# RWKV attention feeding two mixtures of experts, on one core: the attention's small products regrouped by the part of the matmul array they use, and a new hand-written order of the steps

## Chip, core and metric

One NeuronCore of one Trainium2 chip runs the whole program in one launch. The metric is the device time in microseconds (us). Before the change the median of three runs is 1038.5 us.

## What is computed

```python
for t in range(S):                                   # attention, S = 768, 2 batches, 8 heads of 48
    cur = einsum('bhd,bhe->bhde', u[None] * kt, vt)
    y[:, :, t] = einsum('bhd,bhde->bhe', rt, state + cur)
    state = wt[..., None] * state + einsum('bhd,bhe->bhde', kt, vt)
...
P = exp(x @ w_gate - max)                            # first mixture: 8 rounds of row and column
for _ in range(8):                                   # normalisation, then all 8 experts on all rows
    P /= P.sum(1, keepdims=True) + 1e-09; P /= P.sum(0, keepdims=True) + 1e-09; P *= N / E
for e in range(E):
    out += P[:, e:e+1] * (maximum(x @ w1[e], 0) @ w2[e])
...
expert_idx = argmax(xn @ en.T / tau)                 # second mixture: the best expert alone
```

There are 1536 rows of 384 numbers; an expert's two weight matrices are 384 x 1024 and 1024 x 384.

## The kernel before

The attention works in 12 chunks of 128 time steps, six to a batch (`CPB` is 6, so chunks 0 and 6 begin with an empty state). Within a chunk the recurrence is turned into matrix products. Two heads share the 128 partitions: one has partitions 0 to 47, the other 64 to 111, and four such pairs lie side by side.

Each chunk c passes through steps, named in a list by a letter and the chunk's number. `b`, `a` and `c` are DVE work alone (decays by two scans, and the scaled keys `Kt`, queries `Rh` and the product `rp`). The others issue TensorE products:

- `C` (att1d): the bonus term, 16 products with 32 columns of weights each (L639).
- `d` (att2): the scores, 8 products of 48 rows with 128 columns of weights (L654), then 4 transposes of `Kt` (L657); DVE masks the scores into `AT`, ScalarE copies the transposes to `KtT`, GpSimd scales the state `St` to `Tt` (L667).
- `f` (att3): the state's share of the output, 16 products of 48 rows with 64 columns of weights (L679; not in chunks 0 and 6), then the scores' share, 32 products with 32 columns of weights (L686); DVE adds up `x` (L693).
- `z` (att3z): the state's update, 8 products with 48 columns of weights (L718); DVE adds `Tt` and writes `St` (L723).
- `g` (att4): 3 transposes of `x` (L730) and their copies; `h` (att5): the gate's logits, 12 products with 32 columns of weights (L771).

A product of plain float32 operands shows as two rows of weight load and two of matmul in the trace, so `f` issues 64 matmuls from 32 products. The weights of a product are its second operand in the names (`ps<-Rh,Kt`: the weights are `Kt`).

Between these steps stand pieces of the first expert's work for rows whose attention is done: `y` and the digits `1`, `3`, `5`, `7`. They use the whole 128 x 128 array (L274, L294 to L296, L327). `w` is a run of idle-time products on a constant (L541); `i` and `q` split the first expert's weights on ScalarE and DVE; `L` starts the next expert's loads.

The order of everything is written out by hand: the string given to `steps` is the program order, and every engine takes its instructions in that order. PSUM is eight banks that `ps()` hands out.

Of the kernel before, what the change touches and what calls it, by code (L numbers as in the profile page):

```python
# [19 lines left out]
def rwkv_sinkhorn_moe_top1_moe(  # L20
# [527 lines left out]
    NB = 2  # L548
# [59 lines left out]
    def wrk_read(c):  # L608
        wrk_reads[c] = wrk_reads.get(c, 0) + 1
        if wrk_reads[c] == 3:  # L610
            att_load_wrk(c + NB)

    def att1b(c):

        i, suf = c % NB, suft[c % 2]
        nc.vector.tensor_tensor_scan(
            flat(suf)[:, ::-1], wn[i][:, 1:WL + 1][:, ::-1], seg[:, 1:WL + 1][:, ::-1], 0.0,
            op0=ALU.mult, op1=ALU.add,
        )
        nc.vector.reciprocal(segq[c % 2].rearrange("p (a b) -> p a b", b=129)[:, :, 0:1], suf[:, :, 0:1])  # L620
        Kt = a2.tile([128, HP, 128], F32, tag="Kt", name="Kt")
        nc.vector.tensor_tensor(Kt, rk[i][:, 1], suf[:, :, 1:129], ALU.mult)
        st.setdefault(c, {}).update(Kt=Kt, Q=suf[:, :, 0:1])
        wrk_read(c)

    def att1c(c):

# [16 lines left out]
        st[c]["bv"] = bv  # L644

    def att2(c):
        d = st[c]
        Kt, Rh = d["Kt"], d["Rh"]
        AT = a1.tile([128, 2, HP, 128], F32, tag="AT", name="AT")
        aa = [ps(), ps()]  # L650
        for p in range(HP):
            for q in range(2):
                sl = slice(64 * q, 64 * q + D)
                nc.tensor.matmul(aa[q][:, p * 128:(p + 1) * 128], Kt[sl, p, :], Rh[sl, p, :])  # L654
        kk = ps()
        for p in range(HP):
            nc.tensor.transpose(kk[:, p * 128:(p + 1) * 128], Kt[:, p, :], ident)  # L657
        for q in range(2):
            nc.vector.tensor_tensor(
                AT[:, q], aa[q].rearrange("p (a b) -> p a b", b=128),  # L660
                mask.unsqueeze(1).to_broadcast([128, HP, 128]), ALU.mult,
            )
        KtT = a1.tile([128, HP, 128], F32, tag="KtT", name="KtT")
        nc.scalar.activation(out=flat(KtT), in_=kk, func=AF.Copy)
        d["AT"], d["KtT"] = AT, KtT
        if c % CPB:
            nc.gpsimd.tensor_tensor(Tt, St, d["Q"].to_broadcast([128, HP, D]), ALU.mult)  # L667

    def att3(c):
        d = st[c]  # L670
        first = c % CPB == 0
        vv = vn[c % NB]
        y = [ps(), ps()]
        if not first:
            for p in range(HP):
                for t in range(0, 128, 64):
                    for q in range(2):
                        sl = slice(64 * q, 64 * q + D)
                        nc.tensor.matmul(  # L679
                            y[q][t:t + 64, p * D:(p + 1) * D], d["Rh"][sl, p, t:t + 64], Tt[sl, p, :],  # L680
                            start=(p == 0), stop=False,
                        )
        for h in range(H):
            p, q = divmod(h, 2)
            for t in range(0, 128, 32):
                nc.tensor.matmul(  # L686
                    y[q][t:t + 32, p * D:(p + 1) * D], d["AT"][:, q, p, t:t + 32], vv[:, h, :],
                    start=(first and p == 0), stop=(p == HP - 1),
                )
        x = a1.tile([128, DM], F32, tag="x", name="x")  # L690
        by_half = lambda t, q: t.rearrange("p (a b c) -> p b a c", b=2, c=D)[:, q]
        for q in range(2):
            nc.vector.tensor_tensor(  # L693
                by_half(x, q), y[q][:, 0:HP * D].rearrange("p (a c) -> p a c", c=D), by_half(flat(d["bv"]), q), ALU.add
            )
        d["x"] = x
        v_read(c)
        if c % CPB == CPB - 1:
            v_read(c)
# [4 lines left out]
            att_load_rows(c + NB)  # L704

    def att3z(c):
        att3s(c)
        v_read(c)

    def att3s(c):  # L710

        d = st[c]
        vv = vn[c % NB]
        z = ps()
        for p in range(HP):
            for q in range(2):
                sl = slice(64 * q, 64 * q + D)
                nc.tensor.matmul(z[sl, p * D:(p + 1) * D], d["KtT"][:, p, sl], vv[:, 2 * p + q, :])  # L718
        z3 = z[:, 0:HP * D].rearrange("p (a b) -> p a b", b=D)
        for q in range(2):  # L720
            sl = slice(64 * q, 64 * q + D)
# [1 line left out]
                nc.vector.tensor_tensor(St[sl], z3[sl], Tt[sl], ALU.add)  # L723
            else:
                nc.scalar.activation(out=St[sl], in_=z3[sl], func=AF.Copy)

    def split_xT(x, hi, lo, full=None):
        t = ps()
# [513 lines left out]
    with tc.manual_schedule():  # L1242
# [100 lines left out]
        def both(x, y):  # L1343
            return [p + q for p, q in zip(x, y)]

        steps(
# [6 lines left out]
        )  # L1353
        att_stack.close()
        seven = ExitStack()
# [219 lines left out]
```

## Time and profile before

| | |
|---|---|
| median of 3 runs | 1038.5 us (1037.18 to 1038.72) |
| the profiled execution | 1038.07 us, of which the span of the trace is 1036.3 us |
| TensorE busy in the span | 1020.2 us (98%) |
| DVE, ScalarE, GpSimd busy | 681.6, 417.5, 202.7 us |

The attention with the first expert's pieces fills the first 154 us of the span. Times of rows are microseconds from the span's start. `PE` is TensorE's matmul side, `PEld` its weight loads; a matmul's length includes its way through the array, so the time that one product costs is read from the start of one row to the start of the next. "issue" after a wait means that the engine waited for nothing that the profile shows.

### The profile page before, as it was taken

How to read it: one execution, taken by the hardware profiler on the slowest of the kernel's cores; microseconds unless marked ns; L12 is line 12 of the kernel's file. 1: busy time of each engine (PE TensorE's matmuls, PEld its weight loads, DVE VectorE, ACT ScalarE, POOL GpSimd, SP SyncE). 2: the span in 40 equal slices, each digit the busy share in tenths (PEclk: the TensorE clock that was granted, in tenths of full speed). 3: DMA queues.
4: the chain of work that ended last, by engine and by line, in shares of the span. 5: the costliest groups of instructions: out<-in, count | busy, mean ns of one | idle time of the engine just before them, and what ended most of it. 6: DMA issues, size and time to landing. Idle time of an engine off the chain costs nothing.

```text
span 1036.3 us, 20588 instructions
## 1 busy us (share of the span) xinstructions
PE 1020.2 (98%) x8159; PEld 1000.9 (97%) x8159; DVE 681.6 (66%) x1340; ACT 417.5 (40%) x869; POOL 202.7 (20%) x408
## 2 busy tenths in 40 slices
PE   8999999999999999999999999999999999999996
PEld 7899999999999999999999999999999999999996
DVE  7987637765655565566556645655566787987864
ACT  3332233534433343234233323432444544666653
POOL 3111151140110010001001100000054665143201
PEclk9999999999999999999999999999999999999999
DMA  9232201211220122012001101111020324798862
GB/s 241 66 95 69 64 18 32 61 31 32 65 97 1 62 85 78 1 62 62 31 13 56 47 8 31 62 31 62 16 62 1 100 64 126 273 316 272 267 229 71
DMA packets 55785, 87.03 MB, mean 84 GB/s; under 512 B 5355, under 2 KB 48727, under 8 KB 55554
## 3 DMA queue, kind: packets, MB, share of 16 engines
q1 hardware_dynamic: 53056, 80.88, 25.5%
q0 software_dynamic: 2624, 4.75, 1.2%
q8 instruction: 67, 1.10, 0.4%
q14 instruction: 36, 0.29, 0.1%
q10 hardware_dynamic: 2, 0.00, 0.0%
HBM read 75.70 MB, written 13.28 MB: 86 GB/s over the span
## 4 chain that ended last, share of the span: by engine, by line
PE 77%; issue 8%; DVE 6%; DMA 4%; POOL 3%; ACT 1%; POOLq 0%; SPq 0%; DVEq 0%; ACTq 0%
PE ps L518 29%; PE ps L443 25%; PE ps L274 8%; DMA xs<-acc,oidx 4%; PE ps L294 3%; PE ps L296 2%; PE ps L295 2%; PE ps L654 1%; DVE ps L754 1%; PE ps L686 1%; POOL out_dram L1220 1%; POOL xs L1174 1%; PE ps L657 1%; DVE wB L258 1%; PE ps L679 1%
## 5 line engine op out<-in xcount | busy, mean ns | idle before, releaser
L518 PE MATMUL ps<-wA,hh 128*128 128x384 f32 x864 | 221.2, 337 | 0.4 <-ACT hh L458 0.4
L518 PEld LDWEIGHTS ps<-wA,hh 128*128 128x128 f32 x864 | 156.6, 188 | 1.0 <-ACT hh L458 1.0
L522 DVE SCALAR_TENSOR_TENSOR acc<-ps,Pe,acc 128x384 f32<-128x384 f32 x144 | 88.7, 616 | 101.8 <-PE ps L518 101.4
L449 ACT ACTIVATE keep<-ps 128x384 f32<-128x384 f32 x144 | 70.3, 489 | 209.9 <-PE ps L443 208.4
L518 PE MATMUL ps<-wA,hl 128*128 128x384 f32 x432 | 145.8, 337 | 0.1
L459 DVE SCALAR_TENSOR_TENSOR hl<-keep,hh 128x384 fp32r<-128x384 f32 x144 | 81.5, 566 | 91.9 <-ACT hh L458 91.9
L454 DVE TENSOR_TENSOR keep<-ps,keep 128x384 f32<-128x384 f32 x192 | 106.2, 553 | 41.6 <-PE ps L443 36.0
L232 POOL TENSOR_TENSOR stage<-stage 128x128 f32<-128x128 f32 x96 | 49.3, 535 | 421.6 <-DMA stage<-in_moe_w_dram 369.4
L458 ACT ACTIVATE hh<-keep 128x384 fp32r<-128x384 f32 x144 | 75.4, 524 | 123.6 <-DVE keep L454 123.6
L443 PE MATMUL ps<-xTAhi,wA 128*128 128x384 f32 x396 | 101.6, 338 | 0.2 <-ACT keep L449 0.2
L279 ACT ACTIVATE hh<-ps 128x256 fp32r<-128x256 f32 (+1 forms) x128 | 52.9, 416 | 87.5 <-PE ps L274 85.7
L294 PE MATMUL ps<-wA,hh 128*128 128x384 f32 x248 | 85.8, 346 | 0.1
L296 PE MATMUL ps<-wA,hl 128*128 128x384 f32 x248 | 83.2, 335 | 0.0
L295 PE MATMUL ps<-wA,hh 128*128 128x384 f32 x248 | 83.0, 335 | 0.0
L280 DVE SCALAR_TENSOR_TENSOR hl<-ps,hh 128x256 fp32r<-128x256 f32 (+1 forms) x128 | 57.9, 460 | 37.7 <-ACT hh L279 37.3
L518 PEld LDWEIGHTS ps<-wA,hl 128*128 128x128 f32 x432 | 81.1, 188 | 1.3 <-DVE hl L459 1.2
L258 DVE TENSOR_TENSOR wA<-stage,wA 128x768 fp32r<-128x768 f32 (+2 forms) x66 | 73.8, 1122 | 4.1 <-ACT wA L252 3.6
L518 PE MATMUL ps<-slot,hh 128*128 128x384 f32 x288 | 74.0, 338 | 0.0
L252 ACT ACTIVATE wA<-stage 128x768 fp32r<-128x768 f32 (+2 forms) x66 | 62.0, 958 | 27.9 <-POOL stage L232 24.5
L443 PEld LDWEIGHTS ps<-xTAhi,wA 128*128 128x128 f32 x396 | 71.6, 188 | 0.5 <-ACT keep L449 0.5
L443 PE MATMUL ps<-xTAlo,wA 128*128 128x384 f32 x198 | 66.7, 337 | 0.0
L274 PE MATMUL ps<-xTAhi,wA 128*128 128x256 f32 (+1 forms) x336 | 59.0, 311 | 0.0
(329 smaller groups left out, 2084.7 us busy)
## 6 DMA issues: line engine op xcount, KB each, us to landing
stage<-in_moe_w_dram SPq DMA_DIRECT2D x54, 384.0 KB, 3.6
stage<-in_moe_w_dram SPq DMA_DIRECT2D x19, 512.0 KB, 5.2
en<-in_moe_w_dram SPq DMA_DIRECT2D x17, 512.0 KB, 5.2
en<-in_moe_w_dram SPq DMA_DIRECT2D x19, 384.0 KB, 5.0
stage<-in_moe_w_dram SPq DMA_DIRECT2D x28, 256.0 KB, 2.7
rk<-in_wrk_dram SPq DMA_DIRECT2D x24, 192.0 KB, 3.7
stage<-in_moe_w_dram SPq DMA_DIRECT2D x28, 128.0 KB, 2.6
xs<-xz SPq DMA_DIRECT2D x6, 582.0 KB, 4.9
```

The costliest lines, as they stand in the source:

```text
L258: eng.tensor_tensor(out=lo, in0=src, in1=hi.bitcast(F32), op=ALU.subtract)
L274: nc.tensor.matmul(p[:, 0:n], w1_of(g, kk, f)[lo], b[:, kk, :], start=(i == 0), stop=(i == len(mm) - 1))
L294: nc.tensor.matmul(p, hh[:, ts], w2h, start=(f == 0), stop=False)
L295: nc.tensor.matmul(p, hh[:, ts], w2l, start=False, stop=False)
L296: nc.tensor.matmul(p, hl[:, ts], w2h, start=False, stop=(f == KF - 1))
L443: nc.tensor.matmul(t, w, x, start=first_mm and q == 0, stop=q == n - 1, skip_group_check=True,)
L449: nc.scalar.activation(out=t, in_=st_[i][bank][:, 0:384], func=AF.Copy)
L454: nc.vector.tensor_tensor(t, st_[i][bank][:, 0:384], t, ALU.add)
L458: nc.scalar.activation(out=hh, in_=src, func=AF.Relu)
L459: nc.vector.scalar_tensor_tensor(out=hl, in0=src, scalar=0.0, in1=hh.bitcast(F32), op0=ALU.max, op1=ALU.subtract)
L518: nc.tensor.matmul(p, h[:, ts], w, start=n == 0, stop=n == len(mm) - 1)
L522: nc.vector.scalar_tensor_tensor(out=a, in0=p, scalar=P[:, t, e:e + 1], in1=a, op0=ALU.mult, op1=ALU.add)
```

## The change

The state's share of the output moves from `f` into `d`, right behind the scores, as 8 products with 128 columns of weights in place of 16 with 64; its two PSUM banks are taken there. The state's update is cut into parts of 32 and 16 columns, 16 products in place of 8. GpSimd's scaling of the state is issued as soon as both the last chunk's update and this chunk's decays are there (`att_T`). The list of steps is another one.

```diff
+    def att_T(c):
+
+        if c % CPB and "Q" in st.get(c, {}) and "z" in st.get(c - 1, {}):
+            nc.gpsimd.tensor_tensor(Tt, St, st[c]["Q"].to_broadcast([128, HP, D]), ALU.mult)
...
         wrk_read(c)
+        att_T(c)
...
                 nc.tensor.matmul(aa[q][:, p * 128:(p + 1) * 128], Kt[sl, p, :], Rh[sl, p, :])
+        y = d["y"] = [ps(), ps()]
+        if c % CPB:
+            for p in range(HP):
+                for q in range(2):
+                    sl = slice(64 * q, 64 * q + D)
+                    nc.tensor.matmul(
+                        y[q][:, p * D:(p + 1) * D], Rh[sl, p, :], Tt[sl, p, :], start=(p == 0), stop=False,
+                    )
...
-        if c % CPB:
-            nc.gpsimd.tensor_tensor(Tt, St, d["Q"].to_broadcast([128, HP, D]), ALU.mult)
...
-        y = [ps(), ps()]
-        if not first:
-            for p in range(HP):
-                for t in range(0, 128, 64):
-                    for q in range(2):
-                        sl = slice(64 * q, 64 * q + D)
-                        nc.tensor.matmul(
-                            y[q][t:t + 64, p * D:(p + 1) * D], d["Rh"][sl, p, t:t + 64], Tt[sl, p, :],
-                            start=(p == 0), stop=False,
-                        )
...
-                sl = slice(64 * q, 64 * q + D)
-                nc.tensor.matmul(z[sl, p * D:(p + 1) * D], d["KtT"][:, p, sl], vv[:, 2 * p + q, :])
+                for o in range(0, D, 32):
+                    n = min(32, D - o)
+                    sl = slice(64 * q + o, 64 * q + o + n)
+                    nc.tensor.matmul(z[sl, p * D:(p + 1) * D], d["KtT"][:, p, sl], vv[:, 2 * p + q, :])
...
+        v_read(c)
+        d["z"] = True
+        if c + 1 < NCH:
+            att_T(c + 1)
...
-            "b0 c0 a0 w12 b1 w18 w36 C0 d0 w48 i0 c1 a1 i1 f0 i2 q0 q1 z0 w12 q2 d1 C1 w6 g0 i3 q3 z1 f1 y b2 y "
-            "a2 i4 i5 y c2 b3 d2 G0 C2 g1 c3 y f2 a3 y h1 i6 C3 z2 g2 c4 y y q4 h0 d3 h2 1 1 y b4 q5 1 1 C4 f3 q6 "
-            "a4 y c5 z3 1 g3 y 1 d4 b5 1 1 a5 C5 f4 z4 1 1 b6 c6 d5 g4 b7 1 f5 a6 1 h4 3 d6 g5 C6 a7 3 3 3 f6 b8 "
-            "c7 3 z6 3 h3 3 g6 d7 3 3 b9 C7 h6 f7 3 a8 3 3 a9 c8 5 z7 5 h5 5 d8 g7 5 5 C8 5 f8 5 b10 5 g8 5 c9 z8 "
-            "a10 5 C9 d9 5 c10 b11 z9 f9 h7 a11 5 7 d10 7 7 7 z10 7 C10 c11 g9 7 f10 C11 7 d11 g10 h8 7 7 L0 f11 "
-            "h9 7 h10 7 g11 7 "
+            "w6 b0 w6 w36 w6 a0 c0 b1 d0 C0 i0 w12 w24 a1 i1 c1 f0 q0 z0 q1 w12 i2 g0 q2 w12 C1 i3 G0 d1 q3 y z1 "
+            "b2 f1 a2 i5 w12 y w24 c2 y b3 d2 y C2 g1 h0 f2 a3 h1 z2 i6 y y i4 g2 c3 y d3 1 q4 1 C3 q5 f3 z3 q6 "
+            "b4 1 1 y c4 g3 1 y b5 1 1 a4 y 1 1 C4 h2 d4 1 b6 c5 a5 1 z4 f4 a6 C5 d5 c6 g4 b7 1 h4 f5 C6 d6 3 b8 "
+            "3 3 g5 c7 3 3 3 a7 3 3 C7 h3 z6 f6 d7 g6 c8 3 b9 3 3 a8 z7 f7 a9 C8 d8 g7 3 c9 h7 z8 f8 C9 d9 g8 "
+            "b10 c10 5 5 a10 5 5 5 L0 5 5 5 5 b11 h8 C10 z9 h5 f9 h6 d10 5 5 g9 c11 a11 5 7 7 7 7 7 7 7 h9 z10 "
+            "C11 f10 d11 7 g10 7 h10 f11 7 g11 7 7 "
```

Lines of the changed file stand a few lower: scores L661, state's share L667, transposes L672, bonus L645, scores' share L689, update L719, `g` L735, `h` L776.

On TensorE the middle of chunk 8 stood like this before (steps `C8 5 f8`; `xTAhi` and `wA` are the first expert's rows and weights):

```order
L639 MATMUL ps<-ublk,rp 32x2 x16
L274 MATMUL ps<-xTAhi,wA 128x256 x6
L274 MATMUL ps<-xTAlo,wA 128x256 x3
L679 MATMUL ps<-T,Rh 64x48 x16
L686 MATMUL ps<-v_131,AT 32x48 x32
```

and stands like this now, from the last two parts of `z8` through `f8`, `C9` and `d9` to `g8`:

```order
L719 MATMUL ps<-v_131,KtT 32x48
L719 MATMUL ps<-v_131,KtT 16x48
L689 MATMUL ps<-v_131,AT 32x48 x32
L645 MATMUL ps<-ublk,rp 32x2 x16
L661 MATMUL ps<-Rh,Kt 128x128 x8
L667 MATMUL ps<-T,Rh 128x48 x8
L672 MATMUL ps<-ident,Kt 128x128 x4
L735 MATMUL ps<-ident,x 128x128 x3
```

Products of 32 columns now follow each other, then those of 48 rows and 128 columns, then the transposes, with no full-array piece between; the full-array pieces follow in longer runs.

On DVE the state's sum of chunk 7 stands now between two groups of the decays' work (steps `a8 z7 f7 a9 C8 d8`; the scans write `Q`):

```order
L600 SCALAR_TENSOR_TENSOR Q<-w_134,segq_137 128x516
L602 TENSOR_TENSOR Rh<-rk_129,Q 128x512
L724 TENSOR_TENSOR S<-ps,T 48x192 x2
L696 TENSOR_TENSOR x<-ps,bv 128x4x48 x2
L600 SCALAR_TENSOR_TENSOR Q<-w_135,segq_138 128x516
L602 TENSOR_TENSOR Rh<-rk_130,Q 128x512
L674 TENSOR_TENSOR AT<-ps,mask 128x512 x2
```

Before, the same sum of chunk 7 stood between pieces of the expert's work (steps `c8 5 z7 5 h5 5 d8`):

```order
L629 TENSOR_TENSOR rp<-rk_129 128x512
L280 SCALAR_TENSOR_TENSOR hl<-ps,hh 128x256
L723 TENSOR_TENSOR S<-ps,T 48x192 x2
L280 SCALAR_TENSOR_TENSOR hl<-ps,hh 128x256 x2
L659 TENSOR_TENSOR AT<-ps,mask 128x512 x2
```

What moved is the distance from the state's sum to the products that read the scaled state: those were in `f` of the next chunk, and are now in its `d`.

## Rows read from the trace of the kernel before

**Rows 1.** The page: TensorE's busy time, and its instruction queue (packets, MB, share).
```profile
PE 1020.2 (98%) x8159; PEld 1000.9 (97%) x8159; DVE 681.6 (66%) x1340; ACT 417.5 (40%) x869; POOL 202.7 (20%) x408
...
q8 instruction: 67, 1.10, 0.4%
```
**Rows 2.** Windows by stretch: busy PE, PEld, DVE, ACT, POOL, clock, DMA share, GB/s.
```profile
41.46:153.94 112.48, 112.48 (x2102) 104.70 (x2102) 76.61 (x140) 31.87 (x86) 21.38 (x82) 1.00 0.24 61
...
24.60:28.00 3.40, 3.40 (x40) 3.28 (x29) 2.94 (x6) 0.00 (x0) 1.01 (x1) 0.51 0.66 209
```
**Rows 3.** Timeline of TensorE, 90 to 93 us: start, length, operation.
```profile
90.38 0.33 PE L295 MATMUL ps<-wA,hh 128*128 128x384 f32 x1
90.55 0.34 PE L296 MATMUL ps<-wA,hl 128*128 128x384 f32 x1
90.82 0.43 PE L639 MATMUL ps<-ublk,rp 112*32 112x2 f32 x32
91.09 0.38 PE L771 MATMUL ps<-wgT,acc 128*32 128x8 f32 x24
91.40 0.68 PE L679 MATMUL ps<-T,Rh 48*64 48x48 f32 x32
92.01 0.89 PE L686 MATMUL ps<-v,AT 128*32 128x48 f32 x64
92.83 0.44 PE L294 MATMUL ps<-wA,hh 128*128 128x384 f32 x1
93.11 0.34 PE L295 MATMUL ps<-wA,hh 128*128 128x384 f32 x1
```
**Rows 4.** Timeline of TensorE at 145.7 us, a scores' share with gate products behind it.
```profile
145.74 0.89 PE L686 MATMUL ps<-v,AT 128*32 128x48 f32 x64
146.44 0.37 PE L771 MATMUL ps<-wgT,acc 128*32 128x8 f32 x24
```
**Rows 5.** Timeline of TensorE, three kinds of 16 products and a transposing run.
```profile
6.03 0.52 PE L1312 MATMUL ps<-ones,u_sb 1*48 1x1 f32 x16
...
74.52 1.16 PE L654 MATMUL ps<-Rh,Kt 48*128 48x128 f32 x16
75.61 0.66 PE L657 MATMUL ps<-ident,Kt 128*128 128x128 f32 x4
...
82.35 0.56 PE L718 MATMUL ps<-v,KtT 128*48 128x48 f32 x16
```
**Rows 6.** Timeline of TensorE, waits inside runs of small products (idle before, releaser).
```profile
24.39 0.69 PE L686 MATMUL ps<-v,AT 128*32 128x48 f32 x31 [1.44 <-issue]
...
36.03 0.27 PE L639 MATMUL ps<-ublk,rp 112*32 112x2 f32 x12
36.94 0.36 PE L639 MATMUL ps<-ublk,rp 112*32 112x2 f32 x20 [0.64 <-issue]
...
60.08 0.72 PE L718 MATMUL ps<-v,KtT 128*48 128x48 f32 x16
60.73 0.44 PE L294 MATMUL ps<-wA,hh 128*128 128x384 f32 x1
```
**Rows 7.** Windows from 0: TensorE's matmuls and loads (x) up to five moments.
```profile
0.00:18.34 18.34, 16.88 (x349) 16.12 (x349) 13.15 (x26) 6.31 (x11) 6.72 (x42) 1.00 0.88 247
...
0.00:34.02 34.02, 30.65 (x602) 28.12 (x604) 27.73 (x47) 12.38 (x25) 9.88 (x45) 0.95 0.79 209
0.00:36.14 36.14, 32.77 (x730) 29.95 (x730) 29.28 (x51) 13.52 (x28) 10.26 (x45) 0.95 0.74 197
0.00:58.37 58.37, 54.36 (x1110) 49.84 (x1114) 49.55 (x87) 21.54 (x49) 12.96 (x49) 0.97 0.58 150
0.00:60.31 60.31, 56.30 (x1239) 51.65 (x1240) 51.48 (x90) 22.10 (x51) 13.79 (x50) 0.97 0.56 145
```
**Rows 8.** Timeline of DVE and GpSimd: `rp` of chunk 0, a state's sum and its scaling.
```profile
8.39 0.68 DVE L629 TENSOR_TENSOR rp<-rk 128x512 f32<-128x512 f32 x1
...
53.04 0.72 DVE L723 TENSOR_TENSOR S<-ps,T 48x192 f32<-48x192 f32 x2
...
53.93 0.52 POOL L667 TENSOR_TENSOR T<-S,suf 128x192 f32<-128x192 f32 x1 [5.02 <-DVE S L723]
```

More of the change, by code (lines that the diff above doesn't have):

```diff
@@ L665, in att2 @@
         d["AT"], d["KtT"] = AT, KtT
-        if c % CPB:
-            nc.gpsimd.tensor_tensor(Tt, St, d["Q"].to_broadcast([128, HP, D]), ALU.mult)
     def att3(c):
         d = st[c]
-        first = c % CPB == 0
-        vv = vn[c % NB]
-        y = [ps(), ps()]
-        if not first:
-            for p in range(HP):
-                for t in range(0, 128, 64):
-                    for q in range(2):
-                        sl = slice(64 * q, 64 * q + D)
-                        nc.tensor.matmul(
-                            y[q][t:t + 64, p * D:(p + 1) * D], d["Rh"][sl, p, t:t + 64], Tt[sl, p, :],
-                            start=(p == 0), stop=False,
-                        )
+        vv, y = vn[c % NB], d["y"]
         for h in range(H):
@@ L687, in att3 @@
                     y[q][t:t + 32, p * D:(p + 1) * D], d["AT"][:, q, p, t:t + 32], vv[:, h, :],
-                    start=(first and p == 0), stop=(p == HP - 1),
+                    start=(c % CPB == 0 and p == 0), stop=(p == HP - 1),
                 )
@@ L706, in att3z @@
     def att3z(c):
-        att3s(c)
-        v_read(c)
-    def att3s(c):
         d = st[c]
```

## The prediction

> **What bounds the kernel now.** I read the page first: TensorE is busy for 98% of the span [rows 1]. The windows then show that from 41.46 to 153.94 us, where the attention's chunks and the first expert's pieces share the engine, it is busy all the time at full clock, while DVE works for 76.6 of the 112.5 us [rows 2]. So in this stretch the end moves with what TensorE is given to do. Behind it the stages are the same in both programs and wait for nothing of it but its end, so a gain here should come through whole.
>
> Busy is not the same as useful, and the timeline shows why. Between two full-array matmuls of 384 columns there lie 0.17 us from start to start (90.38 to 90.55); before a run of small products it is 0.27 (90.55 to 90.82), and after the run the first full-array matmul takes 0.28 (92.83 to 93.11) [rows 3]. The scores' share of 64 matmuls lasts 0.82 us when a full-array piece follows (92.01 to 92.83), and 0.70 when gate products of the same 32-column kind follow (145.74 to 146.44) [rows 3, 4]. The bonus (32 matmuls) takes 0.27 us ahead of gate products (90.82 to 91.09), while the 24 gate matmuls take 0.31 ahead of a share of another shape: 0.20 at the bonus's rate, and 0.11 more [rows 3]. So each change of the part of the array costs: 0.10 us into a small run, 0.12 + 0.11 = 0.23 from it back to full-array matmuls, and 0.11 between two small shapes.
>
> **The changes saved.** I counted the neighbours on TensorE in both lists from `d2` to the end; transposes next to full-array pieces count as no change. Into small shapes from full-array pieces: 28 before, 11 now. Back: 22 before, 2 now (elsewhere a transposing run comes first). Between small shapes, or between these and transposes: 38 before, 22 now. That is 17 x 0.10 + 20 x 0.23 + 16 x 0.11 = 8.1 us less.
>
> **The state's share.** From `d2` on it occurs nine times. Before, 16 products with 64 columns of weights (32 matmuls) took 0.61 us from 91.40 to 92.01, 0.13 of it the change behind them: 0.48 [rows 3]. Now 8 products (16 matmuls) load 128 columns each. No row has 128 columns of weights under 48 moving ones. Two rows bound it. The scores have the same weights and the same half of the array: 1.09 us for 16 matmuls (74.52 to 75.61), 0.2 of it the change, so 0.9 [rows 5]. The old update has the same 48 moving columns with 48 of weights: 0.56 us from first to last for 16 matmuls, so some 0.36 without the last one's passage [rows 5]. The choice is made by a third row: 16 matmuls with 48 columns of weights and a single moving column last 0.52 [rows 5], hardly less than the 0.56. What is moved doesn't set the time, the weights do, so the share is nearest to the scores: 0.9. It costs 9 x (0.9 - 0.48) = 3.8 us more; with the lower row it would be 1.0 less.
>
> **The update in parts.** 32 matmuls in place of 16. At the rate of the scores' share, 0.70 / 64 = 10.9 ns [rows 4], they take 0.35 us, as much as the old 16 without their passage. I price it at nothing; what it brings is in the changes above. The Trainium skill speaks against it: "TensorEngine Tiling (Array Packing)", section "Instruction Overhead", gives each matmul about 60 cycles whatever it moves. An estimate from that page is 25 ns each at 2.4 GHz, 0.8 us an update and some 4 us in all. The 10.9 ns disagree with it by more than half, so it gets no chance of its own.
>
> **Waits for instructions.** Inside runs of small products the trace has waits that no engine ends: 1.44 us ahead of 24.39, and one ahead of 36.94 that leaves 12 bonus matmuls at 36.03 (0.1 us of work) alone for 0.9, so 0.8 us; the update at 60.08 lasts 0.72 in place of 0.56 [rows 5, 6]. They stand at fixed counts: matmuls and loads up to 18.34, 36.14 and 60.31 us are 698, 1460 and 2479, and the differences are three and four times some 254 [rows 7]. The instruction queue moved 67 packets of 16 KB for about 16,300 such rows, one per 244 [rows 1]. So code comes in blocks of about 256, and the next block wasn't there. The block from 34.02 was used up at 36.13, and the next came 2.9 us after its start; that from 58.37 was used up at 60.31, with 0.15 us to wait, so 2.1 us [rows 6, 7]. In the first case small products led up to the block, in the second a run of full-array matmuls, during which the queue gets ahead.
>
> The new order packs small products closer. `h7 z8 f8 C9` hold 48 + 64 + 128 + 64 = 304 loads and matmuls in 0.2 + 0.35 + 0.7 + 0.27 = 1.5 us, so a block passes in 1.3. Summed in this way along the list, six blocks after `d2` are short: 1.3 (`h7 z8 f8`), 1.5 (`C3 f3 z3`), 2.0 (`z4 f4 C5`), 2.0 (`h4 f5 C6`), 1.9 (`z10 C11 f10`) and 2.6 (`d2` to `f2`). The first four follow full-array pieces: up to 2.1 they wait 0.8 + 0.6 + 0.1 + 0.1. The last two follow small work: up to 2.9 they wait 1.0 + 0.3. That is 2.9 us, against 0.95 before: 2.0 more. With 2.1 for all it would be 1.8 (0.85 more), with 2.9 for all 6.1 (5.1 more).
>
> **The state's sum.** It now has to reach GpSimd and come back before the next `d`'s share. For `z8 f8 C9 d9` TensorE's work in between is 0.7 + 0.4 + 0.9 = 2.0 us. The way is 0.72 for both sums, 0.17 to GpSimd's start and 0.52 there [rows 8]; for the hand-overs from TensorE and back to it I take the same 0.17 each (an estimate from that row). That is 1.75, hidden if DVE takes the sum at once. Only behind `z2` DVE has two groups of earlier work first; I put 0.2 us there.
>
> **The start.** Before `d2` the engines wait for loads and for each other. The scores of chunk 0 no longer stand behind `rp` (0.6 us) [rows 8]. Against that stand one more share, and blocks of code that come as late as before while the weights load. A clock of 1.2 GHz from 24.6 to 28.0 us, behind the wait of 1.44, cost the expert's pieces about 1 us [rows 2, 6]; shorter waits may spare it. Taken: 0.5 less, between nothing and 1.0.
>
> `L` issues the next expert's loads some 30 us earlier; their first use lies after the attention either way, so no time. The loads of `v`, `w` and `rk` move with the steps and have more than a step's time to land.
>
> **Sum.** -8.1 + 3.8 + 0 + 2.0 + 0.2 - 0.5 = -2.6 us. The profiled execution took 1038.07, so it would take 1035.5; the median shown is 0.4 higher, so the forecast is 1035.9.
>
> **Rivals.**
> Code in time. The Trainium skill, "Runtime: NRT & Kernel Launch", section "Instruction fetch mechanics", calls the cost of crossing a block mostly hidden. The wait of 0.8 us at 36 disagrees here, but the other blocks of before wait next to nothing. As a mechanism of this kernel: if the queue gets ahead in the longer full-array runs, the 2.0 vanish and 0.95 is won: 1035.9 - 2.9 = 1033.0. Chance 0.15.
>
> Light weights. If the share follows the old update's 0.36, it gains 1.0 where I have 3.8 lost: 1031.1. Chance 0.08.
>
> No change. If every block takes the 2.9 us seen at 36, the waits are 5.1 and not 2.0 more: 1039.0. For it: the packing makes small work lead up to more blocks. Against it: only one block of the calm stretch was that late. Chance 0.25.
>
> Slower. The state's sum is late. In the new list DVE has the decays' scan and product just ahead of the sum at `a8 z7`, as it often does around it, and in six places (`z4`, `z6` to `z10`) the share is close behind. If DVE is late by one scan and product, 1.3 + 0.6 us less the 0.3 of slack, each place waits 1.6: 6 x 1.6 = 9.6, so 1045.5. It decides from about 0.8 a place on (4.8 - 2.6 = 2.2 above before). Against it: DVE has a third of its time free [rows 2]. Chance 0.1.
>
> **How the numbers follow.** The forecast's own case has 0.42, with 1033.5 to 1038 as its range. A measurement can tell 0.2% (2.1 us) from no change. Faster than 1036.4: three quarters of the forecast's case, both cases below it: 0.31 + 0.15 + 0.08 = 0.54. Slower than 1040.6: 0.1. The rest is 0.36. From 1031.0 to 1039.4 lie the forecast, code in time, no change and half of light weights: 0.86, which is trimmed to 1031.4 at the lower end.
>
> **What would show it.** `C9` behind `f8` without the 0.12 of a change; the share at 0.9 us behind the scores (0.4 if its weights are light); the update at 0.35; waits put down to "issue" inside `f3`, `f8` or `h9 z10 C11`, some 256 rows apart; a clock of 1.0 from 24 to 28 us; GpSimd's `T` ended before the share starts. The forecast is wrong if TensorE waits for `T` in every chunk, or if the runs of small products have no waits for code or twice as many.

## The result, and the profile after

The changed kernel takes 1045.6 us (median of 4 runs, 1043.5 to 1048.9) against 1037.8 for the old one: a ratio of 1.0077, 95% interval 1.0049 to 1.0106. It is slower by about 8 us, where 1035.9 was forecast, with a range of 1031.4 to 1039.4. The profiled execution is the slowest of the four, 1048.9 us with a span of 1046.7, so its parts add up to 3 us more than the median's.

The page shows hardly anything: TensorE is as busy as before, and the queue of instructions moved as many packets [rows 1].

```profile
PE 1025.3 (98%) x8177; PEld 1010.5 (97%) x8177; DVE 680.4 (65%) x1340; ACT 417.6 (40%) x869; POOL 206.4 (20%) x408
...
q8 instruction: 67, 1.10, 0.4%
```

The scores of chunk 2 (`d2`) begin at 36.31 us instead of 30.78, the attention ends at 162.97 instead of 153.94, and 0.9 us more arise behind it, most of it in two places (585 and 904 us) where nothing was edited and which no run here explains. So 5.5 us are lost before `d2` and 3.5 us behind it. The windows of the old kernel and of the changed one, with three stretches of low clock and, as in [rows 7], the counts of matmuls and loads up to four moments:

```profile
30.78:153.94 123.16, 122.52 (x2389) 113.25 (x2389) 86.21 (x157) 37.75 (x103) 23.57 (x85) 1.00 0.24 63
```
```profile
0.00:21.20 21.20, 17.32 (x349) 16.37 (x350) 16.93 (x29) 7.07 (x13) 7.95 (x42) 0.99 0.90 251
0.00:93.00 93.00, 87.06 (x1747) 82.57 (x1748) 72.91 (x128) 30.00 (x73) 18.48 (x54) 0.94 0.44 119
0.00:110.80 110.80, 103.43 (x2127) 98.23 (x2127) 86.39 (x151) 33.95 (x83) 21.23 (x57) 0.95 0.42 113
0.00:148.30 148.30, 139.89 (x2764) 133.88 (x2765) 107.19 (x192) 44.82 (x113) 25.20 (x79) 0.95 0.36 96
36.31:162.97 126.66, 122.17 (x2371) 117.52 (x2370) 85.69 (x157) 38.54 (x103) 24.47 (x85) 0.97 0.23 61
20.60:31.40 10.80, 10.12 (x171) 9.59 (x171) 3.80 (x7) 2.32 (x5) 0.83 (x1) 0.53 0.41 105
112.95:116.40 3.45, 3.45 (x20) 3.40 (x19) 1.32 (x4) 1.45 (x3) 0.00 (x0) 0.51 0.89 296
150.50:153.95 3.45, 3.45 (x16) 3.45 (x16) 0.94 (x2) 1.71 (x4) 0.72 (x1) 0.51 0.00 0
```

From `d2` on TensorE was busy for 122.17 of 126.66 us: it stood still for 4.5 us, where the old kernel lost 0.6. The clock was at 1.2 instead of 2.4 GHz in three stretches; a stretch of 10.8 us at 0.53 of full speed gives away 10.8 x 0.47 = 5.1 us, the other two 1.7 each (an estimate: length times the share of the clock that is missing). The old kernel had one such stretch, worth 1.7 us [rows 2]. What stopped TensorE stands in the list of its waits and in its timeline:

```profile
PE ps L645 <- issue: 4.2, 2, 2.8
PE ps L661 <- issue: 2.7, 2, 1.7
```
```profile
18.23 0.24 PE L645 MATMUL ps<-ublk,rp 112*32 112x2 f32 x8
21.28 0.50 PE L645 MATMUL ps<-ublk,rp 112*32 112x2 f32 x24 [2.81 <-issue]
...
90.31 1.04 PE L661 MATMUL ps<-Rh,Kt 48*128 48x128 f32 x13
93.06 0.38 PE L661 MATMUL ps<-Rh,Kt 48*128 48x128 f32 x2 [1.71 <-issue]
...
108.09 0.52 PE L719 MATMUL ps<-v,KtT 128*32 128x48 f32 x32
108.43 0.86 PE L689 MATMUL ps<-v,AT 128*32 128x48 f32 x64
109.11 0.33 PE L645 MATMUL ps<-ublk,rp 112*32 112x2 f32 x19
110.88 0.30 PE L645 MATMUL ps<-ublk,rp 112*32 112x2 f32 x13 [1.44 <-issue]
...
129.16 0.99 PE L667 MATMUL ps<-T,Rh 48*128 48x48 f32 x16
130.08 0.66 PE L672 MATMUL ps<-ident,Kt 128*128 128x128 f32 x4
...
146.41 0.93 PE L661 MATMUL ps<-Rh,Kt 48*128 48x128 f32 x11
148.35 0.50 PE L661 MATMUL ps<-Rh,Kt 48*128 48x128 f32 x5 [1.01 <-issue]
```

Four runs of equal products break in the middle, with no engine to wait for: in `C1`, `d7`, `C9` and `d11`. Matmuls and loads up to these breaks are 699, 3495, 4254 and 5529; the differences are 11, 3 and 5 times 253 to 255, the same raster as before [rows 7]. This speaks for theory A: code comes in blocks of 256 rows (a row is one matmul or one weight load, and the border between two blocks is called an edge below), a dense run of small products uses a block up before the next is there, and the clock then falls. The trace has the packets of the instruction queue too: one of 16 KB had landed at 19.7, 91.6, 109.6 and 147.0 us, 1.3 to 1.6 us before TensorE went on each time.

The rivals tried against it: B, the new products cost more on TensorE than I priced; C, the state's chain over DVE and GpSimd is late; D, only the start is at fault and the rest a gain.

### The profile page after: what moved, and what is told of

The parts are those of the page before. It is cut to its first block, busy times and chain, and to the rows that moved or that the text cites. A ratio compares the mean times of both kernels' runs of the same rounds, so it can differ in the third digit from the quotient of the medians.

```text
span 1046.7 us, 20632 instructions
## 1 busy us (share of the span) xinstructions
PE 1025.3 (98%) x8177; PEld 1010.5 (97%) x8177; DVE 680.4 (65%) x1340; ACT 417.6 (40%) x869; POOL 206.4 (20%) x408
## 4 chain that ended last, share of the span: by engine, by line
PE 75%; issue 9%; DVE 6%; DMA 4%; POOL 3%; ACT 2%; POOLq 0%; SPq 0%; DVEq 0%; ACTq 0%
PE ps L518 28%; PE ps L443 24%; PE ps L274 8%; DMA xs<-acc,oidx 4%; PE ps L294 2%; PE ps L295 2%; PE ps L296 2%; PE ps L541 1%; PE ps L661 1%; POOL out_dram L1225 1%; DVE ps L759 1%; DVE hl L459 1%; PE ps L667 1%; DVE keep L454 1%; POOL xs L1179 1%
```

## The experiments

Each ratio is to the old kernel run beside it on the same chip, with its 95% interval. Where the texts on record say C8 for the wait near 109 us, the bonus of chunk 9 is meant.

**List and functions apart.** The first kernel has the old functions with the new list, the second the new functions with the old list.

```diff
-            "b0 c0 a0 w12 b1 w18 w36 C0 d0 w48 i0 c1 a1 i1 f0 i2 q0 q1 z0 w12 q2 d1 C1 w6 g0 i3 q3 z1 f1 y b2 y "
...
+            "w6 b0 w6 w36 w6 a0 c0 b1 d0 C0 i0 w12 w24 a1 i1 c1 f0 q0 z0 q1 w12 i2 g0 q2 w12 C1 i3 G0 d1 q3 y z1 "
...
```

> The new list of steps with the old functions (share of the output in f with 64 columns of weights, update uncut, scaling of the state in d). Theory A, code that comes in blocks of 256 rows too late for packed small products: rows per chunk are the same (64 + 32 instead of 32 + 64), so the waits come back, 5 to 6 us of them after d2 and about 3 at C1, and the clock falls behind the long ones: 1045 to 1049 us. Theory B, the new forms cost more on TensorE than I priced: the old forms are back, so about 1038 or less. Theory C, the state's chain over DVE and GpSimd is late in the new place: here the scaled state isn't needed before f, so about 1038.

> The new functions (share in d with 128 columns of weights, update in parts of 32 and 16) with the old list. Theory A: few waits for code, as before (0.7 us), but the dearer share (9 x 0.42 = 3.8 us) and one more change of shape per chunk or none: 1040 to 1042 us. Theory B: the loss is in the forms, so 1045 or more. Theory C: the state's update lies further ahead of the next scores here, so as under A, 1041.

Measured: 1.0029 (1.0016 to 1.0042), median 1041.9, for the list; 1.0044 (1.0028 to 1.0059), 1043.6, for the functions. Their windows from `d2` on, and their low clock:

```profile
33.97:158.51 124.54, 120.14 (x2386) 114.00 (x2386) 85.24 (x157) 38.45 (x103) 24.50 (x85) 0.99 0.24 62
78.00:82.00 4.00, 4.00 (x25) 3.88 (x24) 1.54 (x3) 0.98 (x2) 0.00 (x0) 0.57 0.03 6
```
```profile
36.09:162.23 126.14, 126.14 (x2373) 117.59 (x2374) 87.30 (x158) 36.76 (x100) 24.90 (x85) 0.97 0.25 62
36.00:46.00 10.00, 9.91 (x239) 8.61 (x240) 7.76 (x15) 3.88 (x11) 1.24 (x2) 0.66 0.26 63
```

The list alone brings the waits (124.54 - 120.14 = 4.4 us) without any new form, so B is not their cause, and C isn't either, since the scaled state is needed no earlier here. Its time was expected 3 us too high: its start lost less. The functions alone have no wait behind `d2`; in this profile their loss is a start with a wait of 2.9 us inside idle-time products, where the edge of a block now falls, and the low clock up to 46 us. That last stretch has no wait for code in it; the nearest is one of 1.2 us for DVE just ahead of `d2`. By time both halves cost: 3.4 us the list and 5.0 the functions (1.6 above what A allowed), 8.4 together, where the changed kernel is 7.8 and, run again, 9.9 slower. So the functions cost time too, though they add nothing to TensorE's own work (the table below).

**The start alone.** The changed kernel with the old steps up to `d2`.

```diff
-            "w6 b0 w6 w36 w6 a0 c0 b1 d0 C0 i0 w12 w24 ... b2 f1 a2 i5 w12 y w24 c2 y b3 d2 y C2 g1 h0 f2 ... y y i4 g2 "
+            "b0 c0 a0 w12 b1 w18 w36 C0 d0 w48 i0 c1 a1 ... z1 f1 y b2 y a2 i4 i5 y c2 b3 d2 y G0 C2 g1 h0 f2 ... y y g2 "
```

> The changed kernel with the steps up to d2 in the old order and the new order from there. Theory A: the wait at C1 (2.8 us, and the clock of 1.2 GHz behind it) goes, some 5 us; the blocks' edges then fall on other products, and by the same count there are still 5 to 7 us of waits behind d2, at other products than before the edit: 1039 to 1043 us. Theory D, the start alone is to blame and the packed order behind it is a gain as forecast: 1037 or less. Theories B and C: 1045.

Measured 1.0045 (1.0028 to 1.0063), median 1044.0. In this profile `d2` begins at 31.24; in that of the functions alone, whose program is the same up to `d2`, it was 36.09. So one profile doesn't say what a start costs. The rest is worse:

```profile
31.24:158.58 127.34, 124.59 (x2372) 119.62 (x2373) 86.35 (x158) 37.26 (x100) 24.59 (x85) 0.95 0.24 61
32.00:40.00 8.00, 8.00 (x217) 7.09 (x214) 5.50 (x10) 3.21 (x9) 0.83 (x1) 0.57 0.28 68
108.00:116.00 8.00, 8.00 (x56) 7.91 (x55) 4.11 (x7) 2.22 (x5) 0.00 (x0) 0.57 0.49 156
```

D falls: 2.75 us of waits are left behind `d2`, and 2 x 8 x 0.43 = 6.9 us go to the low clock. By the median it is a little above what A allowed.

**The same work, the edges moved by half a block.** The strongest test, since no step is changed.

```diff
+            nc.tensor.matmul(t[:, 0:k * 128], oneb, oneb.unsqueeze(1).to_broadcast([128, k, 128]))
...
-        warm(W0)
+        warm_long(W0)
...
-            "w6 b0 w6 w36 w6 a0 c0 b1 d0 C0 i0 w12 w24 a1 i1 ...
+            "w6 b0 w6 w36 w6 a0 c0 b1 d0 C0 i0 w12 W24 a1 i1 ...
```

> The changed kernel with 84 of the idle-time products at the start written as 21 products of four times the columns: the same time on the array, but 126 rows of loads and matmuls fewer ahead of everything, half a block. No step from the first scores on is changed. Theory A: the edges of the blocks move by half a block in the program. The waits at C1 (2.8 us), in d7's and d11's scores and in C8 go; waits of 1.5 to 2.5 us appear among the transposes behind z2 (about 42 us) and inside h7's gate products (about 121 us), and nothing of more than 0.5 us elsewhere behind d2: 1039 to 1042 us. Theories B, C and D: the work and the order are the same, so 1045.6 and the waits at the same steps.

Measured 1.0031 (1.0021 to 1.0042), median 1042.3 where the changed kernel was 1.0077 and, run again, 1.0095. The rows behind the first scores are the same, but the waits stand elsewhere, where the count had put them: at 38 us among the transposes behind `z2` (the profile names DVE there, but with the count at 731 + 731 = 1462 it is again an edge, and a packet of code had landed at 38.4, 1.5 us before TensorE went on), and inside `h7`:

```profile
39.91 0.52 PE L743 MATMUL ps<-ident,x 128*128 128x128 f32 x3 [1.06 <-DVE Q L608]
...
119.35 0.20 PE L784 MATMUL ps<-wgT,acc 128*32 128x8 f32 x4
120.91 0.36 PE L784 MATMUL ps<-wgT,acc 128*32 128x8 f32 x19 [1.35 <-issue]
```
```profile
0.00:39.70 39.70, 35.15 (x731) 27.84 (x731) 30.77 (x53) 14.35 (x32) 9.78 (x45) 0.96 0.64 180
...
32.70:153.12 120.42, 118.01 (x2370) 113.56 (x2370) 85.87 (x158) 38.50 (x103) 24.43 (x85) 1.00 0.26 65
```

`d7`, `C9` and `d11` run through. In this profile, which is of the fastest of ten executions (1038.6 us), the clock stays up behind `d2`, and the stretch takes 120.4 us, 2.7 less than in the old kernel.

**How fast code comes.** 512 more products of 32 columns in one run behind the attention of the old kernel; nothing uses them.

```diff
+        p = ps()
+        for r in range(16):
+            for i in range(32):
+                sl = slice(32 * (i % 4), 32 * (i % 4) + 32)
+                nc.tensor.matmul(p[sl, 0:D], ones[:, sl], ident[:, 0:D])
```

> The old kernel with 512 more products of 32 columns of weights and 48 moving ones in one run behind the attention, where the DMA engines are nearly idle; their result is used by nothing. 1024 matmuls and as many loads are 8 blocks of 256 rows. Theory A: at 10.9 ns a matmul a block is used up in 1.4 us, and the next comes 2 to 4 us after the last one, so the run shows a wait every 128 matmuls, 1 to 2.5 us each, and lasts 20 to 30 us in all. Without late code it lasts 11.2 us with no wait in it. The clock should fall to 1.2 GHz in this run if waits and small products bring that about.

```profile
152.49 2.66 PE L1358 MATMUL ps<-ident,ones 128*32 128x48 f32 x228
157.16 2.42 PE L1358 MATMUL ps<-ident,ones 128*32 128x48 f32 x128 [2.01 <-issue]
161.17 2.79 PE L1358 MATMUL ps<-ident,ones 128*32 128x48 f32 x128 [1.59 <-issue]
164.90 1.57 PE L1358 MATMUL ps<-ident,ones 128*32 128x48 f32 x128 [0.94 <-issue]
168.62 1.57 PE L1358 MATMUL ps<-ident,ones 128*32 128x48 f32 x128 [2.16 <-issue]
172.35 1.57 PE L1358 MATMUL ps<-ident,ones 128*32 128x48 f32 x128 [2.16 <-issue]
176.35 1.57 PE L1358 MATMUL ps<-ident,ones 128*32 128x48 f32 x128 [2.43 <-issue]
179.81 0.53 PE L1358 MATMUL ps<-ident,ones 128*32 128x48 f32 x28 [1.89 <-issue]
```
```profile
157.64:164.47 6.83, 4.73 (x231) 4.36 (x220) 0.00 (x0) 0.00 (x0) 0.00 (x0) 0.50 0.02 5
164.47:180.27 15.80, 6.73 (x540) 6.12 (x539) 0.00 (x0) 0.00 (x0) 0.00 (x0) 1.00 0.02 4
158.30:159.75 1.45, 1.28 (x64) 1.09 (x56) 0.00 (x0) 0.00 (x0) 0.00 (x0) 0.50 0.06 11
159.75:161.17 1.42, 0.00 (x1) 0.00 (x1) 0.00 (x0) 0.00 (x0) 0.00 (x0) 0.50 0.00 0
```

The products work for 1.4 us per 128, twice that at the low clock, and then wait. From 157.16 to 179.81 lie six blocks of 128 matmuls and 128 loads: 3.78 us each on average (3.5 to 4.0), with the DMA engines idle (0.02). The 1024 matmuls last 27.8 us instead of 11.2. The low clock of 157.64 to 164.47 ends while the waits go on, so a wait does not have to lower it.

The last two windows show what is waited for. All that moves between 158.30 and 159.75 is one 16 KB packet of the instruction queue, TensorE then stands still with nothing moving, and goes on at 161.17. In this run each packet starts 1.0 to 1.7 us after TensorE took up the block before, takes 0.9 to 1.4, and TensorE goes on 1.3 to 1.6 us after it has landed. The same holds throughout: in this and fifteen other traces of this case, the 43 "issue" waits of over 0.4 us in the first 185 us all end 1.2 to 1.8 us after such a packet has landed. The 3.8 us are no constant, though: behind `d2` of the changed kernel TensorE went on 4.1, 2.9 and 3.3 us after the edge before, and the 254 rows of `C3 f3 z3` passed from 49.15 to 50.57 with no wait, the last packet having landed at 48.5 during full-array pieces.

**Fewer rows by wide products.** Bonus, scores' share, update and gate with 128 columns of weights, with the new list and with the old one (the other three products likewise):

```diff
-            for t in range(0, 128, 32):
-                nc.tensor.matmul(
-                    y[q][t:t + 32, p * D:(p + 1) * D], d["AT"][:, q, p, t:t + 32], vv[:, h, :],
...
+            nc.tensor.matmul(
+                y[q][:, p * D:(p + 1) * D], d["AT"][:, q, p, :], vv[:, h, :],
```

> The changed kernel with the bonus, the scores' share, the update and the gate's logits written as products with 128 columns of weights (4, 8, 4 and 3 products in place of 16, 32, 16 and 12): 228 rows fewer per chunk, the same sums. Theory A (late code, and the clock that falls behind the waits): each product costs some 50 ns a matmul instead of 11, so per chunk about 0.1 + 0.1 + 0.05 + 0.1 us more, 4 us in all; the changes between 32-column parts and full-array pieces go (2 to 4 us back); no waits for code behind d2 (4.5 us back), no fall of the clock there (3.5 us), and at the start at most a small one (up to 5 us): 1034 to 1039 us, and no issue wait over 0.5 us behind d2. If instead the time lies in the products themselves (theory B), it would be slower than the changed kernel, 1047 to 1050.

> The same wide products with the old list of steps. Theory A: what the new list was for (neighbours of one kind) is then had without it, since wide products are full-array pieces: against the old list with the new forms (1043.6 us) the changes of some 4 to 8 us go, 4 us of dearer products come, and the waits at the start shrink (up to 5 us): 1034 to 1041 us. If the order of the steps mattered by more than the changes (state's chain, loads), it would stay 3 us or more behind the wide kernel with the new list.

Measured 1.0429 (1.0409 to 1.0448), 1081.4 us, and 1.0302 (1.0288 to 1.0316), 1069.9: far slower. The price was wrong:

```profile
50.91 0.95 PE L643 MATMUL ps<-ublk,rp 112*128 112x2 f32 x8
51.72 1.96 PE L686 MATMUL ps<-v,AT 128*128 128x48 f32 x16
53.52 1.10 PE L712 MATMUL ps<-v,KtT 128*128 128x96 f32 x8
54.40 0.97 PE L274 MATMUL ps<-xTAhi,wA 128*128 128x256 f32 x6
```
```profile
106.00:120.00 14.00, 14.00 (x87) 13.82 (x87) 6.06 (x11) 2.28 (x6) 1.21 (x2) 0.63 0.20 53
```

(From 51.72 to 53.52 lie 1.80 us for 16 matmuls.) A float32 matmul with 128 x 128 of weights takes 0.10 to 0.11 us whether it moves 2, 48 or 96 columns, where four parts of 32 columns take 4 x 0.011. There is no wait for code in either kernel, as A says. But the clock of the first falls often, here for most of 14 us in which TensorE never waits; some 3 us of these products lead up to it. So the experiment doesn't separate the theories by its time, and it shows that waits are not the only thing that the clock falls behind.

**The changed kernel once more.**

> The changed kernel once more, unchanged, since its first profile was of its slowest execution (1048.9 us of 1043.5 to 1048.9). Theory A: the waits for code stand at the same products (C1, d7, C8, d11), since they follow from counts; how often the clock falls behind them may differ from run to run, by 1.7 us for each fall of 3.4 us. Median 1043 to 1046.

Median 1047.5, ratio 1.0095 (1.0080 to 1.0111). The waits are in the same four steps (`C1`, `d7`, `C9`, `d11`, 5.1 us in all). The clock was low in other stretches, so the waits are fixed by counts and the clock scatters.

**An order without short blocks.** Full-array pieces moved between the small products until, at 3.8 us a block, the count shows no wait; idle-time products written long to put the edges where the order wants them. Beside it the same order with the edges elsewhere, the old kernel with the same edges, and the order with the old functions.

```diff
-... c3 y d3 1 q4 1 C3 q5 f3 z3 q6 b4 1 1 y c4 g3 1 y b5 1 1 a4 y 1 1 C4 h2 d4 1 b6 c5 a5 1 z4 f4 a6 C5 ...
+... c3 y d3 1 1 q4 C3 q5 f3 z3 q6 1 b4 1 y c4 g3 1 y 1 b5 1 a4 y C4 h2 d4 1 b6 1 c5 a5 1 z4 f4 1 a6 C5 ...
...
-... w18 w36 C0 d0 w48 i0 ...
+... w18 w36 C0 d0 W48 i0 ...
```

> The changed kernel's functions with the old steps up to d2 and a new order behind it: small products stay beside their own kind, but full-array pieces are moved (the order among them kept) so that none of the blocks of 256 rows is used up before the next can be there, counted with 3.8 us from one block to the next as in the run of 1024 small products. 108 of the idle-time products at the start are written as 27 of four times the columns, which puts the blocks' edges 162 rows later in the program. Theory A: no wait for code over 0.3 us behind d2, and with no such wait hardly a fall of the clock there. From d2 to the end of the attention 116 to 118 us (old kernel 123.2, changed kernel 126.7), so 1031 to 1034 us in all. If the waits are not what costs the time, 1040 or more, as with the new list before.

> The same order of steps with all idle-time products at the start written as in the old kernel, so the blocks' edges fall 162 rows earlier in the program; nothing else differs. Theory A: by the count some 6 to 8 us of waits come back, in h1 or z2 (1.3 us), d9 or C9 (1.6), h6 or f9 (2.4), d11 (2.0), and the clock may fall behind them: 1038 to 1043 us. If alignment doesn't matter, the same as its partner.

> The old kernel with the same 108 idle-time products written as 27 long ones, no other edit. Theory A: its two waits for code behind d2 (1 us) go and at the start they move; 1035 to 1038 us. It shows what of the gain of the spread order is had by the shift alone: at most 2 us.

> The spread order and the long idle-time products with the old functions (share of the output in f with 64 columns, update uncut). In five profiles the stretch from d2 on, less waits and time lost to the low clock, is 118 to 119 us with the new list whatever the forms, so the forms should hardly matter; by the count this one has 1 to 2.4 us of waits for code, late in f9 or C10: 1033 to 1037 us. If the new forms are what makes the order pay, 1038 or more.

Measured: 1.0137 (1.0118 to 1.0157), 1052.1 us; unshifted 1.0173 (1.0155 to 1.0190), 1055.7; the old kernel with long products 0.9996 (0.9986 to 1.0007), 1037.2; old functions 1.0067 (1.0044 to 1.0090), 1045.6. Only the third came as expected. The waits for code did go, but others came; the longest of the spread order's waits behind `d2`:

```profile
PE ps L669 <- DVE Rh L610: 4.3, 3, 3.4
```
```profile
56.00:64.00 8.00, 6.29 (x45) 6.20 (x46) 2.91 (x4) 0.60 (x1) 0.00 (x0) 0.57 0.30 75
```

No "issue" stands among them. I had moved the pieces of chunks 3 to 5 ahead of the decays, DVE was late by up to 3.4 us, and behind that wait the clock fell as it does behind the others. The unshifted partner had 1.7 us of waits for code behind `d2`, where the count had 6 to 8, beside the same waits for DVE; in its profile the low clock took 12 us there instead of 5, and its median is 3.7 us higher. So the count at 3.8 us a block foretells too many waits where TensorE waits for something else as well.

**Fewer moves.** Ten pieces moved, all behind `d7`; beside it the new list as it is with the same edges.

```diff
-... c8 3 b9 3 3 a8 z7 f7 a9 C8 d8 g7 3 c9 h7 z8 f8 C9 d9 g8 b10 c10 5 5 a10 5 5 5 L0 5 5 5 5 b11 h8 C10 z9 h5 f9 h6 ...
+... c8 3 b9 3 a8 z7 f7 a9 C8 3 d8 g7 3 c9 h7 z8 f8 C9 d9 g8 b10 c10 5 5 5 a10 5 5 L0 5 5 5 b11 h8 C10 z9 5 5 h5 f9 h6 ...
...
-... w18 w36 ...
+... W18 w36 ...
```

> The changed kernel's functions, the old steps up to d2, the new list behind it with ten full-array pieces moved, all of them behind d7 (the spread order before moved them ahead of the decays' work of chunks 3 to 5, and TensorE then waited 3 us and more for DVE), and 78 idle-time products at the start as 20 long ones: edges 116 rows later. By the count no wait for code over 0.3 us behind d2. Theory A: no wait for DVE over 0.5 us either, so from d2 to the end of the attention 116.5 to 119 us where the clock stays up (old 123.2), up to 2 us more for each fall of the clock: 1032 to 1036 us. If the new list costs time by something else than code, DVE and the clock that falls behind such waits, 1038 or more.

> The same with the new list as it is, no piece moved; only the edges lie as in its partner. Theory A: by the count two waits for code are left behind d2, about 1.0 us in h3 or z6 (near 94 us) and 2.4 us in h7 (near 116 us), none at d7, C8 or d11: 3 us more than its partner, and perhaps one fall of the clock (2 us): 1035 to 1041 us.

Measured 1.0019 (1.0010 to 1.0028), 1039.9, and 1.0042 (1.0026 to 1.0059), 1042.6. Behind `d2` the first comes near what A says (116.5 to 119 us):

```profile
33.30:152.91 119.61, 118.76 (x2373) 114.14 (x2373) 86.12 (x158) 36.76 (x100) 23.26 (x83) 1.00 0.26 65
```

That is 3.6 us less than the old kernel. But the edge in `C1` waited 2.4 us again, DVE was late by 2.0 behind it, and `d2` began 2.5 us later; a further 2.5 arose behind the attention, most of it between 898 and 905 us. So its time is 4 us above what A allowed. The partner has one of the two waits that the count foresaw (1.9 us in `h7`), the clock fell behind it, and it is 2.7 us slower.

**The start without that wait.** The same functions with the edges 206 rows later (138 idle-time products written as 35, not 120 as 31 as the text on record has it) and pieces moved to fit them, and with 24 idle-time products behind `d2` to bring the edges back.

```diff
-... w12 b1 W18 w36 C0 d0 w48 ...
+... W12 b1 W18 w36 C0 d0 W48 ...
```
```diff
-... w18 w36 C0 d0 w48 i0 ... d2 y G0 C2 ...
+... w18 w36 C0 d0 W48 i0 ... d2 y w12 w12 G0 C2 ...
```

> Like the kernel with ten pieces moved, but with other idle-time products at the start written long (120 as 31), so that the edges fall 206 rows later than in the old start, and pieces moved behind chunk 5 to fit these edges. By the count one wait of 0.6 us behind d2 (in C6). Theory A: 117 to 119.5 us from d2 on where the clock stays up; the start decides the rest, from 30 us (no wait for code there) to 34 (a wait of 2.4 us in a bonus): 1033 to 1038 us. If the new order costs time by something else, 1039 or more again.

> The order with ten pieces moved, with the start of the run whose scores of chunk 2 began at 30.1 us (edges 162 rows later), and 24 idle-time products (1.3 us of TensorE) put behind d2 to bring the edges back to the place for which the order was made. By the count no wait over 0.3 us behind d2. Theory A: start 30 to 31 us, then 118 to 120.5 us (1.3 of it the idle-time products): 1033 to 1037 us. If the new order costs time by something else, 1039 or more.

Measured 1.0001 (0.9986 to 1.0017), 1038.5, and 0.9993 (0.9980 to 1.0005), 1037.2 us. The second's profiled execution took 1036.0:

```profile
29.80:150.77 120.97, 120.07 (x2397) 115.49 (x2397) 86.21 (x158) 36.91 (x100) 23.25 (x83) 1.00 0.25 65
```

The attention ends 3.2 us earlier than in the old kernel, of which 2.1 are left at the end. Over twelve runs the time is the same, since they scatter: at a mean granted clock of 0.997 or more it took 1035.2 to 1037.8 us, at 0.992 or 0.993 1040.5 and 1041.2. The old kernel, run 23 times beside it, was below 0.995 only twice. No version has beaten the old kernel by more than a measurement can tell.

Theory A told where TensorE would stand better than how long a kernel would take. Of the fifteen times forecast from it, one came inside its range (the old kernel with long products), one below, and thirteen above, three of these by 0.5 us or less.

## Why the prediction was wrong

Two terms failed: the clock, which the sum behind `d2` put at nothing, and the start, which had the wrong sign. The waits for code were put too low and partly in the wrong places. The work saved was right in size.

**TensorE's own work: right.** From `d2` to the attention's end, less TensorE's idle time and what the low clock took:

| kernel | length | idle | low clock | rest |
|---|---|---|---|---|
| old | 123.2 | 0.6 | 0 | 122.5 |
| old list, new functions | 126.1 | 0 | 3.4 | 122.7 |
| changed | 126.7 | 4.5 | 3.4 | 118.8 |
| new list, old functions | 124.5 | 4.4 | 1.7 | 118.4 |
| old start, new list | 127.3 | 2.8 | 6.9 | 117.7 |
| edges moved | 120.4 | 2.4 | 0 | 118.0 |
| ten pieces moved | 119.6 | 0.8 | 0 | 118.8 |

The changes saved and the dearer share were -8.1 + 3.8 = -4.3; the changed kernel shows 118.8 - 122.5 = -3.7. The rows agree one by one: `f8` takes 0.68 us from 108.43 to 109.11 with no change to `C9`, the update 0.34 (108.09 to 108.43), the share 0.92 with its change (129.16 to 130.08). What the sum hid is that the list brings the gain and the functions nothing: with either list they move the rest by less than 1 us. By time they cost 5 to 7 us in each of the three pairs that differ in them alone (ratios 1.0044 against 1 with the old list, 1.0077 and 1.0095 against 1.0029 with the new one, 1.0137 against 1.0067 in the spread order), and the mean clock is lower each time (0.994 against 0.997, 0.9905 against 0.995, 0.989 against 0.994). Why is open.

**Waits for code: right mechanism, wrong size.** "2.0 more" came from 2.1 us (2.9 behind small work) from one block to the next. The run of 1024 products gives 3.8, and the three waits behind `d2` came 4.1, 2.9 and 3.3 us after the edge before. Behind `d2` TensorE stood still for 4.5 us instead of 0.6, so 3.9 more, inside the bounds of 0.85 and 5.1 that I had. Of the six short blocks named two waited: the one from `h7` to `C9` (1.44 us, taken 0.8) and the one behind `h9 z10 C11` (1.01, taken 1.0). The other four had no wait, and the longest, 1.71 in `d7`, was not named. I had looked for the densest rows in the list; which block is short depends on where the edges fall, and moving them by 126 rows moved the waits. The Trainium skill ("Runtime: NRT & Kernel Launch", "Instruction fetch mechanics") calls the crossing of a block mostly hidden. The 1024 products disagree: 7 crossings cost them 13 us.

**The clock: not in the sum.** I had it only at the start, as something that shorter waits might spare. It took 5.1 + 1.7 + 1.7 = 8.5 us in the profiled execution against 1.7 before, more than the waits did. It isn't one execution's bad luck: the eight timed runs of the changed kernel have mean clocks of 0.989 to 0.992 (mean 0.9905), nine of the old one beside them 0.996 to 0.998 (0.9969). The difference, 0.64% of 1040 us, is 6.7 us, most of the 7.8 to 9.9 measured.

**The start: wrong sign.** Taken 0.5 less; it was 5.5 more, and 2.6 in the second profile of the changed kernel, where `d2` begins at 33.40. In the first, the clock cost 5.1 us instead of 1.7, which is 3.4 of it. The edge at row 699 fell into `C1`, a dense run while the weights load, and TensorE waited 2.8 us, where the old kernel waited 0.5 at the same edge in `d1` and 1.44 in `f1` [rows 6]; with the other waits its idle time ahead of `d2` is 4.0 us instead of 3.4, so 0.6. The last 1.5 are work, 1.0 of it 18 more idle-time products. "Blocks come as late as before" was so (6.1 us from the edge before to `C1`'s, 5.0 and 5.3 in the old kernel), but it looked at when code comes and not at which products an edge would meet. The scores of chunk 0 won nothing (they start at 11.03 us, 11.00 before), and "one more share" is none, since that of chunk 1 stood ahead of `d2` in the old kernel too.

**The state's sum: right.** No wait for GpSimd's `T` is among TensorE's waits of the changed kernel, so the slower rival, which came nearest in time (1045.5), did so by luck: it had the wrong cause. None of the rivals had the waits and the clock together. "A gain here should come through whole" did not quite hold either: 0.9 us arose behind the attention here, 2.5 with ten pieces moved.

So the sum behind `d2` is -3.7 + 3.9 + 3.4 = +3.6 (measured 3.5), not -2.1. What makes the clock fall stays open. It fell after waits for code, after a wait for DVE, and in the wide kernel with no wait at all; it stayed up after the wait of 1.7 us in `d7`, and in the long run it rose again while TensorE waited more than half the time.

## What to carry to other kernels

Count the rows of weight loads and matmuls, not only their time: where small products use up 256 of them in less than some 3 to 4 us, the next block of code may be waited for (with several such blocks in a row it was, every 3.8 us), and packing them closer then gains nothing. Where the edges fall is part of the schedule, and any edit ahead of them moves it, so look at several positions before judging an order. In these runs a wait on TensorE cost its length and often again as much in the clock behind it, so an order that saves tenths at each change of shape pays only if it adds no wait.

## What was unexpected

In one long run of small products code comes at only 256 rows in 3.8 us even with idle DMA engines (0.02): the packet itself takes some 1.2 of it, the rest passes before its start and after its end. A float32 matmul with 128 x 128 of weights takes 0.10 to 0.11 us whether it moves 2, 48 or 96 columns; with 48 rows of weights it is some 0.05 (16 in 0.92 us with the change behind them), and in parts of 32 columns 0.011. The same program differs by up to 7 us from run to run (1034.9 to 1042.0 with the edges 206 rows later), and the mean granted clock mostly goes with it.
